# Attention plus MLP on one core: where a weight transfer is waited for, and which score product opens a filled half step

## The chip, the cores and the metric

The kernel runs on one core of a Trainium2 chip. The metric is the device time of one execution in microseconds (us), taken as the median of several runs; lower is better. The kernel before takes 1595.82 us (three runs, 1595.52 to 1599.61).

## The reference

One transformer block with a conditioning vector `c`, for 2048 rows of 512 numbers. Every head shares one key and one value of width 16 (multi-query attention, 32 heads).

```python
mod = (_silu(c) @ w_mod).reshape(c.shape[0], 6, 1, -1)
sa, ca, ga, sb, cb, gb = ...
h = _layernorm(x) * (1 + ca) + sa
q = (h @ wq) -> 32 heads of 16;  k = h @ wk;  v = h @ wv
scores = einsum("bhqd,bkd->bhqk", q, k) * (Dh ** -0.5)
x = x + ga * ((softmax(scores) @ v) @ wo)
h = _layernorm(x) * (1 + cb) + sb
x = x + gb * (gelu(h @ w1 + b1) @ w2 + b2)
```

## The kernel before

**Units and half steps.** The 2048 query rows are cut into 8 blocks of 256. A unit is one block and one group of four heads, so there are 64 units, worked through in order. For each unit every score is computed twice. A *max product* (`m`, line 490, in `Max.step`) is a score product whose 128x512 result VectorE reduces to a row maximum (line 495); a unit's maxima are found some units ahead and written into the unit's query tile as extra rows. An *exp product* (`e`, line 571, in `sexp`) is the same score with the maximum subtracted; ScalarE takes its exponential into `p` (line 572). Then `pv` (line 583) multiplies `p` by the values, for four heads side by side. One pass of the main loop does two key steps X and Y. It is cut in two halves, each a mix of score products closed by one `pv`; that stretch, from one `pv` to the next, is called a half step here. There are 512, and a counter `clock[0]` goes up by two in each (`due()` runs what was put off to a count by `later`).

**The two lanes.** A score product uses only 64 of TensorE's 128 rows: `s` = 0 or 1 names which. So each half step has two lanes, issued as two groups by `issue`: it always takes the next product of the group whose length so far is smaller, the first group on a tie. Each engine gets its instructions in exactly that written order (`manual_schedule`).

**Plain and filled half steps.** A plain half step (`plain`) has exp and max products in both lanes. A filled half step has four max and three exp products in one lane (call it A), and in the other (B) the halves of a batch of other work followed by the fourth exp product. That other work is the projections: `qps` for the queries, `wops` behind the attention, `tp` transposes, `w1ps` and `w2ps` of the MLP, all through `half` (line 183). A batch is split by rows, so the first half step of a pair runs the one 64-row half of it and the second the other. The second's group ends with `resume`, which lets the job that owns the batch go on: if an accumulation has ended, this writes the VectorE instruction that empties its PSUM bank. In the kernel before, where the batch ends an accumulation, the reduction of lane A's third max product is held back (`hold`) until `resume` has written that instruction.

**PSUM banks.** Max products rotate over three banks (tag `m`), so a max product must wait until the reduction of the one three before it is done. Exp products use three banks `e0`, `e1`, `e2`; lane A uses them in that order and lane B's exp product uses `e0` again, so it waits until the half step's first exponential is done.

**Weights of the MLP.** `fetch_w1` (line 732) moves one 512 KB piece of `w1` from DRAM into one of three buffers, by a DMA issued by SyncE. Three pieces are fetched ahead; piece f+3 is asked for one count after the last product of piece f. In the kernel before, the first product of a piece (in lane B) is what waits for it. One piece is used in each pair of half steps.

Of the kernel before, what the change touches and what calls it, by code (L numbers as in the profile page):

```python
# [11 lines left out]
ALU = mybir.AluOpType  # L12
AX = mybir.AxisListType

P = 128
# [27 lines left out]
def raw(ap):  # L43
    return ap.bitcast(F32)
# [3 lines left out]
def adaln_mqa_mlp(  # L48
# [15 lines left out]
    nc = tc.nc  # L64
# [41 lines left out]
    ks = const.tile([P, S], F32R, name="ks")  # L106
# [7 lines left out]
    dw1 = tc.dram_tile([NF, P, 2, KD, P], F32, name="dw1")  # L114
# [22 lines left out]
    clock = [0]  # L137
# [310 lines left out]
    NU = len(units)  # L448
    qsts = {}

    def load_q(u):

        b, Q = units[u]
        r0, w = blocks[b]
        qst = qsts[u] = qbufs[u % QBUFS]
        h, g, a0 = r0 // BQ, Q // 2, (Q % 2) * 2
        cols = slice(r0 % BQ, r0 % BQ + w)
        assert (h, g) in sent
        for s in range(2):
            for r, part in ((0, 0), (16, 1), (32, 0)):  # L460
                nc.sync.dma_start(out=raw(qst[64 * s + r:64 * s + r + 16]), in_=dq[h][g][part, a0 + s][:, :, cols])
            if u >= QBUFS:
                nc.sync.dma_start(out=raw(qst[64 * s + 48:64 * s + 50]), in_=dz)

    class Max:
# [14 lines left out]
        def has(self, s):  # L480
            return bool(self.todo[s])

        def step(self, s, hold=None, **place):
            u, j, t, kc = self.todo[s].pop(0)
            T = blocks[units[u][0]][1] // P
            if u not in self.mx:
                self.mx[u] = att.tile([P, 4 * T, NKC], F32, name=f"mx{u}", tag="mx", bufs=2)
            m = psum.tile([P, 512], F32, name=f"m{u}_{j}_{t}_{kc}_{s}", **(place or dict(tag="m", bufs=3)))
            rows = slice(64 * s, 64 * s + 64)
            nc.tensor.matmul(m, qsts[u][rows, j, t * P:(t + 1) * P], ks[rows, kc * 512:(kc + 1) * 512],  # L490
                             start=True, stop=True)
            i = (s * 2 + j) * T + t

            def reduce():
                nc.vector.tensor_reduce(out=self.mx[u][:, i, kc:kc + 1], in_=m, axis=AX.X, op=ALU.max)  # L495
                self.left[u] -= 1
                if self.left[u] == size[u] // 2 and u > 1 and u + 1 < NU:
                    load_q(u + 1)
                if self.left[u] == 0:
                    put_max(u, self.mx.pop(u))  # L500

            self.done += 1
            if hold is None:
                reduce()
            else:
                hold.append(reduce)

    placed = set()
    mms = []
# [44 lines left out]

    ptiles = {}
    accs = {}

    def sexp(u, K, j, s, bank):

        w = blocks[units[u][0]][1]  # L560
        qst = qsts[u]
        assert u in placed
        if (u, K) not in ptiles:
            ptiles[u, K] = att.tile([P, 2, 2, 512], F32, name=f"p{u}_{K}", tag="p", bufs=3)
        e = psum.tile([P, 512], F32, name=f"e{u}_{K}_{j}_{s}", tag="x" if bank == "x" else f"e{bank}", bufs=1)
        rows = slice(64 * s, 64 * s + 64)
        if w == 512:
            kt, rhs = K, qst[rows, j, :]
        else:
            kt, rhs = 2 * K + j, qst[rows].rearrange("p j n -> p (j n)")  # L570
        nc.tensor.matmul(e, ks[rows, kt * P:(kt + 1) * P], rhs, start=True, stop=True)  # L571
        nc.scalar.activation(ptiles[u, K][:, j, s, :], e, AF.Exp, scale=0.25)  # L572

    def pv(u, K):
# [154 lines left out]

    def fetch_w1(b, w1ts, f):  # L730
        w1ts[f] = wts_pool["rest"].tile([P, 2, KD, P], F32R, name=f"w1t{b}_{f}", tag="w1t", bufs=3)
        nc.sync.dma_start(out=raw(w1ts[f]), in_=dw1[f])

    def fetch_rest(b):

# [335 lines left out]
    held = []  # L1071

    def go_on(job):
        r = next(job[1], None)
        holder[:] = [job] if isinstance(r, list) or r is not None and r <= 0 else []
        if r is None:
            queue.remove(job)
        elif isinstance(r, list):
            held.append(r)
        else:  # L1080
            job[0] = clock[0] + max(abs(r), 1)
        return r is not None

    def resume():

        go_on(holder[0])
# [12 lines left out]
    def take():  # L1099
        advance()  # L1100
        return held.pop() if held else None

    size = [4 * (blocks[b][1] // P) * NKC for b, _ in units]
    first = [sum(size[:u]) for u in range(NU + 1)]
    mp = Max()
# [79 lines left out]
    rows = xhat1(1, act)  # L1185
# [49 lines left out]
    def products(batch):  # L1235

        return sum(b_.shape[-1] * (4 if b_.dtype == F32 else 1) for _, _, b_, _, _ in batch) / 512
# [7 lines left out]
    def issue(*groups):  # L1245

        at = [0.0] * len(groups)
        groups = [list(g) for g in groups]
        while any(groups):
            g = min((g for g in range(len(groups)) if groups[g]), key=lambda g: at[g])  # L1250
            length, fn = groups[g].pop(0)
            fn()
            at[g] += length

    def mixture(a, b):

        out = []
        while a or b:
            if a:
                out.append(a.pop(0))  # L1260
            if b:
                out.append(b.pop(0))
        return out
# [10 lines left out]
    for u in range(NU):  # L1274
        for K in range(0, steps[u], 2):
            goal = lead[u] + (lead[u + 1] - lead[u]) * (K + 2) / steps[u]
            goal = min(goal, first[u + QBUFS] if u + QBUFS < NU else first[NU])
            n = max(0, 2 * round((goal - mp.done) / 2))

            def maxes(s, n, first_=1.0, held=None):  # L1280
                return [(1.0 if i else first_, lambda i=i: mp.step(s, held if i == 2 else None)) if mp.has(s) else (0.0, lambda: None)
                        for i in range(n)]

            def exps(s, which):
                return [(1.0, lambda K=K, j=j, bank=bank: sexp(u, K, j, s, bank)) for K, j, bank in which]

            def halves(batch, s):

                total = products(batch)
                ahead = AHEAD if total > BATCH - 0.5 else (BATCH - (1.5 if batch[-1][4] else 0.5)) / total  # L1290
                return [(ahead * products([one]), lambda one=one: half(one, s)) for one in batch]

            def plain(s, K, t, n, banks):

                a, b_, c_, d = banks
                one = mixture(exps(s, [(K, 0, a), (K, 1, c_)]), maxes(s, n))
                other = maxes(t, n)
                if not holder and mp.has(t) and n > 1:
                    other[-1] = 1.0, lambda: mp.step(t, tag="x", bufs=1)
                issue(one, exps(t, [(K, 0, b_)]) + other + exps(t, [(K, 1, d)]))  # L1300

            X, Y = K, K + 1
            due()
            batch = take() if behind else None
            if batch:
                issue(mixture(maxes(1, n // 2, 0.0), exps(1, [(X, 0, 0), (X, 1, 1), (Y, 0, 2)])),
                      halves(batch, 0) + exps(0, [(X, 0, 0)]))
            else:  # L1310
                plain(1, X, 0, (n + 2) // 4, (1, 2, 0, 1))
            clock[0] += 1
            due()
            if behind:
                end_step(*behind)
            clock[0] += 1
            due()
            if batch:

                reduces = [] if batch[-1][4] else None  # L1320

                def go_on_():
                    resume()
                    for fn in reduces or ():
                        fn()

                issue(mixture(maxes(0, n // 2, 0.0, reduces), exps(0, [(X, 1, 0), (Y, 0, 1), (Y, 1, 2)])),
                      halves(batch, 1) + [(0.0, go_on_)] + exps(1, [(Y, 1, 0)]))
                advance()
            else:  # L1330
                plain(1, Y, 0, n // 4, (2, 0, 1, 2))
            clock[0] += 1
            due()
            end_step(u, X)
            behind = (u, Y)
            clock[0] += 1
            if state["mods"] and state["q"] == 0 and w2H is None:
                w2H = att.tile([P, NF, D], F32R, name="w2H", tag="bigH")
                w2L = att.tile([P, NF, D], F32R, name="w2L", tag="bigL")
                preps["w2"] = prep_w2()  # L1340
            if clock[0] >= prepared[0] + PREP and weights and weights[0] in preps:
                prepared[0] = clock[0]
                if next(preps[weights[0]], 0) == 0:
                    weights.pop(0)
# [51 lines left out]
```

## Time and profile before

| | us |
|---|---|
| median of the runs | 1595.82 |
| the profiled execution, whole | 1597.31 |
| its span on the core | 1595.0 |
| TensorE busy | 1569.6 |
| VectorE busy | 1410.1 |
| ScalarE busy | 1203.6 |
| GpSimd busy | 668.1 |

The span is the part between the first and the last instruction; 2.3 us of the profiled execution lie around it. In the profile PE is TensorE's matmuls, PEld its weight loads, PEq or PEldq its sequencer, DVE VectorE, ACT ScalarE, POOL GpSimd and SP SyncE. A row of the timeline gives start, duration, engine, line, operation, the output and inputs by the program's names, and shapes; "x2" means that two such instructions in a row are merged, and brackets give the idle time ahead of it with what ended it. Half steps run from about 79 us to 1540 us of the span.

### The profile page before, as it was taken

To read this page: it belongs to the slowest core of one execution; us is meant where nothing else is said; L and a number is where in the kernel's file an instruction comes from. 1 tells how busy PE (TensorE), PEld (TensorE's weight loads), DVE (VectorE), ACT (ScalarE), POOL (GpSimd) and SP (SyncE) were. 2 spreads that over 40 slices of the span, in tenths; PEclk is the share of its full clock that TensorE was granted. 3 is DMA by queue.
4 is the path that set the end of the run, shared out by engine and by line. 5 is a ranking of instruction groups with operands and counts; after the bars stand their busy time and mean duration, and the time that the engine had idled before them with its cause. 6 is when DMAs were issued, how large, how long until landed. Compare 5 with 4: busy or idle time off the path is not lost.

```text
span 1595.0 us, 41579 instructions
## 1 busy us (share of the span) xinstructions
PE 1569.6 (98%) x16369; PEld 1020.0 (64%) x16369; DVE 1410.1 (88%) x2473; ACT 1203.6 (75%) x2393; POOL 668.1 (42%) x1176
## 2 busy tenths in 40 slices
PE   6999999999999999999999999999999999999998
PEld 3466665557666676657666676656666676666667
DVE  6899999899989998999999999899999999999615
ACT  5577777778777887778877887778877887778853
POOL 4445443757412571246512562234602474225711
PEclk9999999999999999999999999999999999999999
DMA  7235312413021220303112120303112120211232
GB/s 242 88 109 198 121 65 70 133 32 108 14 78 51 60 78 26 102 19 106 32 48 80 54 85 22 105 15 98 43 36 91 43 97 18 95 40 61 83 132 74
DMA packets 83126, 121.62 MB, mean 76 GB/s; under 512 B 19614, under 2 KB 56222, under 8 KB 82676
## 3 DMA queue, kind: packets, MB, share of 16 engines
q1 hardware_dynamic: 82916, 118.97, 22.9%
q8 instruction: 129, 2.11, 0.6%
q14 instruction: 65, 0.53, 0.1%
q10 hardware_dynamic: 16, 0.00, 0.0%
HBM read 91.13 MB, written 27.27 MB: 74 GB/s over the span
## 4 chain that ended last, share of the span: by engine, by line
PE 92%; DVE 4%; ACT 2%; DMA 1%; POOL 0%; issue 0%; SPq 0%; ACTq 0%; DVEq 0%; POOLq 0%
PE acc L583 31%; PE m L490 25%; PE e L571 18%; PE w1ps L183 7%; PE w2ps L183 4%; DVE mx L495 3%; PE wops L183 1%; PE w2ps L177 1%; PE qps L183 1%; PE w1ps L177 1%; ACT p L572 1%; PE kps L159 1%; PE tp L183 1%; ACT h L838 0%; PE modr L279 0%; DMA wm<-in_w_mod_dram 0%
## 5 line engine op out<-in xcount | busy, mean ns | idle before, releaser
L495 DVE TENSOR_REDUCE mx<-m 128x1 f32<-128x512 f32 x2048 | 1269.0, 681 | 106.0 <-PE m L490 80.8
L572 ACT ACTIVATE p<-e 128x512 f32<-128x512 f32 x2048 | 1069.5, 599 | 307.5 <-PE e L571 237.1
L490 PE MATMUL m<-ks,qst 64*128 64x512 f32 x2048 | 820.4, 424 | 6.5 <-ACT ks L393 2.4
L571 PE MATMUL e<-qst,ks 64*128 64x512 f32 x2048 | 743.1, 407 | 2.9 <-ACT p L572 1.5
L583 PE MATMUL acc<-p,va 128*32 128x256 f32 x8192 | 548.0, 385 | 0.0
L490 PEld LDWEIGHTS m<-ks,qst 64*128 64x128 f32 x2048 | 362.7, 184 | 226.2 <-DVE mx L495 138.4
L571 PEld LDWEIGHTS e<-qst,ks 64*128 64x128 f32 x2048 | 365.9, 184 | 86.5 <-ACT p L572 59.0
L583 PEld LDWEIGHTS acc<-p,va 128*32 128x32 f32 x8192 | 213.8, 109 | 219.2 <-issue 115.8
L183 PE MATMUL w1ps<-h2H,w1t 64*128 64x256 f32 x1232 | 235.1, 287 | 0.0
L539 POOL TENSOR_SCALAR mt<-turned 8x32 f32<-8x32 f32 x256 | 53.5, 209 | 397.0 <-DVE turned L545 385.0
L183 PEld LDWEIGHTS w1ps<-h2H,w1t 64*128 64x128 f32 x1232 | 184.2, 185 | 0.0
L183 PE MATMUL w1ps<-h2L,w1t 64*128 64x256 f32 x616 | 169.7, 276 | 0.0
L183 PE MATMUL w2ps<-w2H,gH 64*128 64x512 f32 x286 | 117.8, 412 | 0.0
L183 PE MATMUL w2ps<-w2H,gL 64*128 64x512 f32 x286 | 117.3, 410 | 0.0
L183 PE MATMUL w2ps<-w2L,gH 64*128 64x512 f32 x286 | 117.3, 410 | 0.0
L183 PEld LDWEIGHTS w1ps<-h2L,w1t 64*128 64x128 f32 x616 | 113.5, 184 | 0.0
L891 POOL TENSOR_SCALAR tt<-tt 128x256 f32<-128x256 f32 x77 | 31.3, 406 | 163.0 <-ACT tt L890 159.5
L892 POOL TENSOR_TENSOR tt<-tt,z 128x256 f32<-128x256 f32 x77 | 57.0, 740 | 6.4
L134 POOL TENSOR_TENSOR gL<-z,gH 128x256 fp32r<-128x256 f32 x77 | 56.9, 739 | 6.4
L902 POOL TENSOR_TENSOR z<-tt,z 128x256 f32<-128x256 f32 x77 | 56.5, 734 | 6.0
L901 POOL TENSOR_TENSOR tt<-tt,z 128x256 f32<-128x256 f32 x77 | 56.7, 736 | 0.0
L183 PEld LDWEIGHTS w2ps<-w2H,gH 64*128 64x128 f32 x286 | 52.7, 184 | 0.6
(188 smaller groups left out, 1468.6 us busy)
## 6 DMA issues: line engine op xcount, KB each, us to landing
w1t<-dw SPq DMA_DIRECT2D x82, 512.0 KB
qst<-dq SPq DMA_DIRECT2D x384, 32.0 KB
do<-oc SPq DMA_DIRECT2D x64, 128.0 KB
dw<-w1s SPq DMA_DIRECT2D x11, 512.0 KB
xt<-in_A_x_dram SPq DMA_DIRECT2D x4, 1024.0 KB
dq<-qH SPq DMA_DIRECT2D x16, 256.0 KB
dq<-qL SPq DMA_DIRECT2D x16, 256.0 KB
x<-in_A_x_dram SPq DMA_DIRECT2D x8, 512.0 KB
```

The costliest lines, as they stand in the source:

```text
L134: eng_l.tensor_tensor(out=dst_l, in0=src, in1=raw(dst_h), op=ALU.subtract)
L177: nc.tensor.matmul(ps, a, b_, start=first_, stop=last_)
L183: nc.tensor.matmul(ps, a[rows], b_[rows], start=first_ and s == 0, stop=last_ and s == 1)
L490: nc.tensor.matmul(m, qsts[u][rows, j, t * P:(t + 1) * P], ks[rows, kc * 512:(kc + 1) * 512], start=True, stop=True)
L495: nc.vector.tensor_reduce(out=self.mx[u][:, i, kc:kc + 1], in_=m, axis=AX.X, op=ALU.max)
L539: nc.gpsimd.tensor_scalar(out=mt[:, g:g + 32], in0=turned[g:g + 4 * T, :], scalar1=1.0, scalar2=0.0, op0=ALU.mult, op1=ALU.add)
L571: nc.tensor.matmul(e, ks[rows, kt * P:(kt + 1) * P], rhs, start=True, stop=True)
L572: nc.scalar.activation(ptiles[u, K][:, j, s, :], e, AF.Exp, scale=0.25)
L583: nc.tensor.matmul(accs[u][32 * cidx:32 * cidx + 32, :], va[:, kt, :], rhs, start=kt == 0, stop=kt == NKT - 1)
L892: nc.gpsimd.tensor_tensor(out=tt, in0=tt, in1=z, op=ALU.mult)
L901: nc.gpsimd.tensor_tensor(out=tt, in0=tt, in1=z, op=ALU.mult)
L902: nc.gpsimd.tensor_tensor(out=z, in0=tt, in1=z, op=ALU.add)
```

## The change

Three things. First, lane A of a filled half step begins with an exp product and alternates exp, max, exp, max, exp, max, max; before, it was max, exp, max, exp, max, exp, max. Second, the holding back of a reduction is gone. Third, a transfer of a `w1` piece is noted with a count six higher than the present one (`heed`), and from that count on the next exp product with `s == 0` and an odd key step in the second half of a pair waits for it (`wait_early`), one transfer for each such product, in the order of the transfers.

```diff
-        def step(self, s, hold=None, **place):
+        def step(self, s, **place):
...
-            def reduce():
-                nc.vector.tensor_reduce(out=self.mx[u][:, i, kc:kc + 1], in_=m, axis=AX.X, op=ALU.max)
...
-            if hold is None:
-                reduce()
-            else:
-                hold.append(reduce)
+            nc.vector.tensor_reduce(out=self.mx[u][:, i, kc:kc + 1], in_=m, axis=AX.X, op=ALU.max)
...
+    def heed(dma, n):
+        heeded.append((clock[0] + n, dma.ins.name))
+
+    def wait_early(ins):
+        if heeded and heeded[0][0] <= clock[0]:
+            tc.add_manual_dep(ins.ins, heeded.pop(0)[1], ...)
...
-        nc.tensor.matmul(e, ks[rows, kt * P:(kt + 1) * P], rhs, start=True, stop=True)
+        ins = nc.tensor.matmul(e, ks[rows, kt * P:(kt + 1) * P], rhs, start=True, stop=True)
+        if clock[0] % 4 == 2 and s == 0 and K % 2:
+            wait_early(ins)
...
-        nc.sync.dma_start(out=raw(w1ts[f]), in_=dw1[f])
+        heed(nc.sync.dma_start(out=raw(w1ts[f]), in_=dw1[f]), 6)
...
-            def maxes(s, n, first_=1.0, held=None):
-                return [(1.0 if i else first_, lambda i=i: mp.step(s, held if i == 2 else None)) ...]
+            def maxes(s, n):
+                return [(1.0, lambda: mp.step(s)) if mp.has(s) else (0.0, lambda: None) for i in range(n)]
...
-                issue(mixture(maxes(1, n // 2, 0.0), exps(1, [(X, 0, 0), (X, 1, 1), (Y, 0, 2)])),
+                issue(mixture(exps(1, [(X, 0, 0), (X, 1, 1), (Y, 0, 2)]), maxes(1, n // 2)),
                       halves(batch, 0) + exps(0, [(X, 0, 0)]))
...
-                issue(mixture(maxes(0, n // 2, 0.0, reduces), exps(0, [(X, 1, 0), (Y, 0, 1), (Y, 1, 2)])),
-                      halves(batch, 1) + [(0.0, go_on_)] + exps(1, [(Y, 1, 0)]))
+                issue(mixture(exps(0, [(X, 1, 0), (Y, 0, 1), (Y, 1, 2)]), maxes(0, n // 2)),
+                      halves(batch, 1) + [(0.0, resume)] + exps(1, [(Y, 1, 0)]))
```

More of the change, by code (lines that the diff above doesn't have):

```diff
@@ L492, in step @@
             i = (s * 2 + j) * T + t
-            def reduce():
[L495 to L500, printed above, removed]
-            self.done += 1
-            if hold is None:
-                reduce()
-            else:
-                hold.append(reduce)
+            nc.vector.tensor_reduce(out=self.mx[u][:, i, kc:kc + 1], in_=m, axis=AX.X, op=ALU.max)
+            self.done += 1
+            self.left[u] -= 1
+            if self.left[u] == size[u] // 2 and u > 1 and u + 1 < NU:
+                load_q(u + 1)
+            if self.left[u] == 0:
+                put_max(u, self.mx.pop(u))
     placed = set()
@@ L556, in adaln_mqa_mlp @@
     accs = {}
+    heeded = []
+    def heed(dma, n):
+        heeded.append((clock[0] + n, dma.ins.name))
+    def wait_early(ins):
+        if heeded and heeded[0][0] <= clock[0]:
+            tc.add_manual_dep(ins.ins, heeded.pop(0)[1], mybir.DependencyInfo(mybir.DependencyClass.Sync, mybir.DependencyReason.DATA),
+                              reason="a weight piece")
     def sexp(u, K, j, s, bank):
@@ L1278, in adaln_mqa_mlp @@
             n = max(0, 2 * round((goal - mp.done) / 2))
-            def maxes(s, n, first_=1.0, held=None):
-                return [(1.0 if i else first_, lambda i=i: mp.step(s, held if i == 2 else None)) if mp.has(s) else (0.0, lambda: None)
-                        for i in range(n)]
+            def maxes(s, n):
+                return [(1.0, lambda: mp.step(s)) if mp.has(s) else (0.0, lambda: None) for i in range(n)]
             def exps(s, which):
@@ L1318, in adaln_mqa_mlp @@
             if batch:
[L1320 to L1325, printed above, removed]
-                issue(mixture(maxes(0, n // 2, 0.0, reduces), exps(0, [(X, 1, 0), (Y, 0, 1), (Y, 1, 2)])),
-                      halves(batch, 1) + [(0.0, go_on_)] + exps(1, [(Y, 1, 0)]))
+                issue(mixture(exps(0, [(X, 1, 0), (Y, 0, 1), (Y, 1, 2)]), maxes(0, n // 2)),
+                      halves(batch, 1) + [(0.0, resume)] + exps(1, [(Y, 1, 0)]))
                 advance()
```

## The prediction

> **What bounds the kernel now.** I read the page first: the engines' shares and the chain that ended last.
>
> ```profile
> PE 1569.6 (98%) x16369; PEld 1020.0 (64%) x16369; DVE 1410.1 (88%) x2473; ACT 1203.6 (75%) x2393; POOL 668.1 (42%) x1176
> ...
> PE 92%; DVE 4%; ACT 2%; DMA 1%; POOL 0%; issue 0%; SPq 0%; ACTq 0%; DVEq 0%; POOLq 0%
> ...
> L495 DVE TENSOR_REDUCE mx<-m 128x1 f32<-128x512 f32 x2048 | 1269.0, 681 | 106.0 <-PE m L490 80.8
> L572 ACT ACTIVATE p<-e 128x512 f32<-128x512 f32 x2048 | 1069.5, 599 | 307.5 <-PE e L571 237.1
> ```
>
> TensorE is the chain (92%), but VectorE is close behind it, nearly all of it reductions. A busy share can't say whether a half step is as short as TensorE can make it, so I went on to the windows of the `pv` line and then to the timeline of single half steps. First the rate, and a plain half step, which begins with exp products already:
>
> ```profile
> 600.00:800.00 200.00, 74.95 (x1120) 29.21 (x1120) 1.00 0.18 57
> ```
>
> ```profile
> 686.40 1.07 PE L583 MATMUL acc<-p,va 128*32 128x256 f32 x16
> 687.40 0.50 PE L571 MATMUL e<-qst,ks 64*128 64x512 f32 x2
> ...
> 689.01 0.42 PE L583 MATMUL acc<-p,va 128*32 128x256 f32 x4
> ```
>
> 1120 `pv` matmuls at 16 a half step are 70 half steps in 200 us, at a full granted clock (1.00). Six of them are plain; this one takes 689.01 - 686.40 = 2.61 us, and counting all six so the 64 filled ones take (200 - 15.7) / 64 = 2.88 us. Now a filled one, by engine:
>
> ```profile
> 802.90 1.07 PE L583 MATMUL acc<-p,va 128*32 128x256 f32 x16
> 803.90 0.50 PE L490 MATMUL m<-ks,qst 64*128 64x512 f32 x1
> 803.95 0.50 PE L183 MATMUL w2ps<-w2H,gL 64*128 64x512 f32 x1
> 804.24 0.39 PE L571 MATMUL e<-qst,ks 64*128 64x512 f32 x1
> ...
> 804.69 0.39 PE L571 MATMUL e<-qst,ks 64*128 64x512 f32 x1
> ...
> 805.15 0.66 PE L571 MATMUL e<-qst,ks 64*128 64x512 f32 x2
> 805.39 0.38 PE L490 MATMUL m<-ks,qst 64*128 64x512 f32 x1
> 805.74 0.84 PE L583 MATMUL acc<-p,va 128*32 128x256 f32 x10
> ```
>
> ```profile
> 804.43 0.69 DVE L495 TENSOR_REDUCE mx<-m 128x1 f32<-128x512 f32 x1 [0.35 <-PE w2ps L183]
> ```
>
> ```profile
> 804.66 0.60 ACT L572 ACTIVATE p<-e 128x512 f32<-128x512 f32 x1 [0.77 <-PE e L571]
> ```
>
> ```profile
> 805.18 0.18 PEld L490 LDWEIGHTS m<-ks,qst 64*128 64x128 f32 x1
> 805.31 0.18 PEld L571 LDWEIGHTS e<-qst,ks 64*128 64x128 f32 x1
> ```
>
> `pv` takes 1.00 us until the first score product; the second of lane A starts 0.34 later and the others every 0.23; 0.35 after the last start comes the next `pv`. That is 2.84 us, with little slack in two places. The fourth max product needs the bank of the first: product ends 804.40, reduction 804.43 to 805.12, weights loaded at 805.18, only 0.03 after the product ahead of it began, which is the earliest they can be. And lane B's exp product needs the first exponential: 804.66 to 805.26, weights at 805.31.
>
> **The change part by part.** In the written order VectorE, ScalarE and GpSimd keep every instruction in its place; only TensorE's order and its waits move. 436 of the 512 half steps are filled ones with max products, and all 436 change in the same way.
>
> *Exp first.* The entry costs the same with either product first: 1.00 us from `pv` in the plain half step and in the filled one. So nothing is won there. But the first max product moves to the second place, and the fourth stays last. The first then starts at 0.34 and ends 0.39 later (as the second product does now), at 0.73 from the first score product instead of 0.50; VectorE starts 0.04 behind it (804.40 to 804.43), at 0.77, and ends 0.69 later, at 1.46. The fourth's weights follow 0.06 behind (805.12 to 805.18): 1.51, where now they are loaded at 1.28. There are no more than three banks, so nothing hides this. A half step of before shows what it costs, one in which VectorE was late for another reason:
>
> ```profile
> 728.14 1.07 PE L583 MATMUL acc<-p,va 128*32 128x256 f32 x16
> 729.14 0.49 PE L490 MATMUL m<-ks,qst 64*128 64x512 f32 x1
> ...
> 731.07 0.42 PE L583 MATMUL acc<-p,va 128*32 128x256 f32 x4
> ```
>
> ```profile
> 729.91 0.69 DVE L495 TENSOR_REDUCE mx<-m 128x1 f32<-128x512 f32 x1 [0.17 <-PE e L571]
> ```
>
> ```profile
> 730.65 0.18 PEld L490 LDWEIGHTS m<-ks,qst 64*128 64x128 f32 x1
> ```
>
> Its reduction starts at 0.77, the weights are loaded at 1.51, and the next `pv` follows 0.42 later: 2.93 us. That is the new filled half step. The gain on the other side, exponentials 0.23 to 0.34 earlier and so lane B's exp product free at 1.18 instead of 1.41, lies beside the later end of lane A and is worth nothing. Against the mean of 2.88 the loss is 0.05 to 0.06 us x 436 = 24 us.
>
> *Knock-on.* Reductions that follow on one another take 1269.0 / 2048 = 0.62 us each. Four from 0.77 on (0.69 + 3 x 0.62) keep VectorE until 3.32, that is 0.39 into the next half step's products, and 0.38 more fits ahead of its first reduction without harm. Where a longer instruction comes in between, that reduction is late:
>
> ```profile
> L778 DVE BATCH_NORM_STATS2 st<-x 128x6 f32<-128x512 f32 x16 | 10.9, 682 | 0.1
> L938 DVE TENSOR_TENSOR ot<-w2ps,x 128x512 f32<-128x512 f32 x16 | 11.1, 691 | 23.6 <-PE w2ps L183 15.9 <-PE w2ps L177 7.8
> L771 DVE TENSOR_TENSOR x<-wops,x 128x512 f32<-128x512 f32 x16 | 11.0, 690 | 2.4 <-PE m L490 1.6 <-PE wops L177 0.8
> L441 DVE COPY q<-qps 128x512 f32<-128x512 f32 x14 | 9.7, 692 | 0.2
> ```
>
> ```profile
> 678.93 0.68 DVE L778 BATCH_NORM_STATS2 st<-x 128x6 f32<-128x512 f32 x1
> ```
>
> Before, four reductions from 0.53 on end at 3.08, 0.24 into the next products (half step 2.84); 0.68 for the instruction, 0.69 for the reduction and 0.06 give weights at 1.67. After it is 0.39 instead of 0.24: 0.15 later, where the main term has counted 0.055. So these 62 cases (one of them at 678.93) cost 0.095 more each: 6 us. It may be nothing, if VectorE catches up during work that it waits for, or 12, if each case delays a second half step.
>
> *The hold.* The reduction held back now stands behind what empties lane B's bank without it, since the third max product is itself written later; VectorE's order is unchanged: 0.
>
> *The early wait.* What it adds is a wait on an exp product; behind it stand the rest of the half step and `pv`, so a late piece would stop TensorE. When do pieces land?
>
> ```profile
> 553.53 0.28 PE L183 MATMUL w1ps<-h2L,w1t 64*128 64x256 f32 x1
> ```
>
> ```profile
> 556.82 3.20 SPq L732 DMA_DIRECT2D w1t<-dw  x2
> ...
> 1475.48 0.82 SPq L732 DMA_DIRECT2D w1t<-dw  x2
> ```
>
> ```profile
> 557.80:558.80 1.00, 1.00 (x16) 0.85 (x13) 0.54 (x2) 0.44 (x3) 0.83 (x3) 1.00 0.95 287
> 558.80:559.70 0.90, 0.90 (x14) 0.75 (x10) 0.90 (x2) 0.90 (x3) 0.62 (x1) 1.00 0.74 278
> ```
>
> Here the last product of a piece began at 553.53, and the next fetch into its buffer was issued at 556.82, since SyncE had other transfers to issue first. The two windows (DMA share 0.95 and 0.74, 287 GB/s for 1.0 us and 278 for 0.9) move 0.54 MB, a whole piece: it lands by about 559.8, 3.0 after its issue. The new wait stands seven counts after the asking, some 3.5 half steps or 10 us: 563.5. Slack 3.7 us even here. The worst is the pair at 1475.48 in the last block, which lands at 1478.5; its wait is the third score product of the half step at 1476.31 (below), so at 1476.31 + 1.00 + 0.57 = 1477.9: 0.6 us late, once. The rules of "DMA: Bandwidth & Descriptors" in the Trainium skill (section Rules for kernel authors) say to wait on a transfer's semaphore late; by that rule this part can only lose, and by the rows above it loses no more than that 0.6 us.
>
> What it takes away is a second wait at a piece's first product, handled by a sequencer instruction of its own:
>
> ```profile
> L183 PEldq EVENT_SEMAPHORE  x9: 51/51/51, 714.8 to 772.5; - x9
> ```
>
> ```profile
> 1476.31 1.07 PE L583 MATMUL acc<-p,va 128*32 128x256 f32 x16
> ...
> 1477.32 0.50 PE L183 MATMUL w1ps<-h2H,w1t 64*128 64x256 f32 x2
> ...
> 1479.16 1.07 PE L583 MATMUL acc<-p,va 128*32 128x256 f32 x16
> ...
> 1480.30 0.47 PE L183 MATMUL w1ps<-h2H,w1t 64*128 64x256 f32 x2
> ```
>
> A piece's first product starts 1.14 us after its `pv`, that of the other half 1.01 after: lane B loses 0.13. For about 59 pieces that is 0 to 8 us. I take 0, because lane A now ends later than lane B and covers it.
>
> Sum: 24 + 6 + 0 + 0 = +30 us. On the profiled execution 1597.31 becomes 1627.3; its own time is 1.5 above the median of the runs, so 1595.82 becomes 1626.
>
> **The rivals.**
>
> *Program order holds the max products (3%).* In 336 half steps lane B's exp product is now written ahead of the third and the fourth max product. If TensorE starts matmuls strictly as written, these two wait for it: it starts behind six halves, at 0.34 + 5 x 0.23 = 1.5, the third max product not before that, the last 0.23 later and `pv` another 0.35 later, at 2.08. That is 3.08 for the half step, 0.20 above today's: 67 us for these 336 and 6 for the other 100, so 1669. Against it: the first `w2ps` at 803.95 starts ahead of the exp product at 804.24, which is written before it. "TensorE: Matmul & The Clock Gate" in the Trainium skill (Part 3, What overlaps and what doesn't) has matmuls in strict order of start and end; this trace has them out of order between the two lanes.
>
> *VectorE's lateness adds up (12%).* If the 0.1 of the knock-on is the rule and not the exception, because the small reductions and copies push as well, the loss is 0.1 x 436 = 44 us: 1640. For it: VectorE's 88%. Against it: the longer half step leaves VectorE 0.38 us of air.
>
> *Exponentials decide, not banks: faster (7%).* The place is lane B's exp product, which waits for ScalarE at 1.41 today; in most half steps the fourth max product stands behind it in order. If that wait is what ends half steps, freeing it 0.23 earlier brings filled half steps from 2.88 towards 2.82 (1.00 + 0.34 + 5 x 0.23 + 0.33), and the early wait adds its 8 us on the w1 half steps: up to 26 + 8, and half of it gives 1579. This decides if the fourth max product's weights are loaded before 1.41; the bank's chain above gives 1.51.
>
> *Hidden (6%).* Lane B ends at 2.86 to 2.9 in w1 half steps anyway; if `pv` could start its own weights while the last max product streams, the delay would vanish: 1596. Against it stands the half step at 728.14.
>
> **How the numbers follow.** The forecast has 72%; the rivals have 12 (adding up), 7 (faster), 6 (hidden) and 3 (program order). The forecast's own range comes from the main term at 0.04 to 0.07 us (17 to 31), the knock-on's 0 to 12 and the early wait's -8 to +1: 1605 to 1640. To leave out no more than 2 in 10 I take 1607 to 1645, with the adding-up rival inside. A change of 0.3% (5 us) is about what can be told from none: faster 0.08, same 0.06, slower 0.86.
>
> **What would show it.** Right: rows of filled half steps with the first reduction 0.77 us after the first score product, the fourth max product's weights at 1.51, `pv` to `pv` at 2.93; 68 instead of 70 half steps in 200 us; VectorE's busy time unchanged and its idle time up by some 30 us; the first `w1ps` product of a piece 1.01 after `pv`; plain half steps at 2.61. Wrong: weights of the fourth max product at or below 1.41; an exp product idle for a DMA; `pv` above 3.0.

## The result, and the profile after

| | before | after |
|---|---|---|
| median of four runs each (us) | 1596.76 (1595.52 to 1599.61) | 1639.18 (1637.88 to 1640.67) |
| span of the profiled execution (us) | 1595.0 | 1635.6 |
| TensorE busy (us) | 1569.6 | 1607.8 |
| VectorE busy (us) | 1410.1 | 1412.1 |
| the 436 filled half steps, summed (us) | 1259.9 | 1303.8 |

The change makes the kernel slower: the ratio of the time after to the time before is 1.0263, with a 95% interval of 1.0245 to 1.0281. That is 42 us, where 30 were forecast. The last row is worked out from the `pv` rows of the two timelines. The filled half steps lose 43.9 us, so they hold all of the loss; the rest of the span is 3.3 us shorter. In the twelve traces of this document that rest lies between 331.1 and 336.7 us and goes with no part of the change; the time up to the first `pv` alone lies between 80.7 and 84.9 us.

The page of the changed kernel, its engines, the chain of waits and the group of reductions (in this kernel `pv` is line 588, the exp product 574, the reduction 493):

```profile
PE 1607.8 (98%) x16369; PEld 1025.2 (63%) x16369; DVE 1412.1 (86%) x2473; ACT 1224.4 (75%) x2393; POOL 665.1 (41%) x1176
...
PE 88%; DVE 7%; DMA 2%; POOL 1%; ACT 1%; issue 0%; SPq 0%; DVEq 0%; POOLq 0%; ACTq 0%
...
L493 DVE TENSOR_REDUCE mx<-m 128x1 f32<-128x512 f32 x2048 | 1277.9, 684 | 146.0 <-PE m L490 96.3
```

TensorE is still 98% busy, with 38 us more of it for the same 16369 matmuls. The busy share hides the loss: in the half step shown below no matmul has idle time ahead of it, but the fourth max product is busy for 0.47 us, where the one in the prediction's half step of before is for 0.38. What moved are the shares of the chain (VectorE 4% to 7%) and the idle time ahead of reductions (106.0 to 146.0 us). VectorE does the same work and waits 40 us longer for it.

The rate, from the windows of the `pv` line:

```profile
600.00:800.00 200.00, 72.90 (x1092) 28.38 (x1088) 1.00 0.17 56
```

1088 weight loads at 16 a half step are 68 half steps in 200 us, as forecast. One filled half step with `w1ps` work in lane B, on the timelines of TensorE, of its weight loads and of VectorE:

```profile
924.22 1.07 PE L588 MATMUL acc<-p,va 128*32 128x256 f32 x16
925.22 0.50 PE L574 MATMUL e<-qst,ks 64*128 64x512 f32 x1
...
925.56 0.39 PE L490 MATMUL m<-ks,qst 64*128 64x512 f32 x1
...
926.75 0.47 PE L490 MATMUL m<-ks,qst 64*128 64x512 f32 x1
927.15 1.07 PE L588 MATMUL acc<-p,va 128*32 128x256 f32 x16
```

```profile
926.73 0.18 PEld L490 LDWEIGHTS m<-ks,qst 64*128 64x128 f32 x1
```

```profile
925.99 1.29 DVE L493 TENSOR_REDUCE mx<-m 128x1 f32<-128x512 f32 x2 [0.34 <-PE m L490]
```

From the first score product at 925.22: the first max product starts at 0.34, its reduction at 0.77, and the weights of the fourth max product are loaded at 1.51. `pv` to `pv` takes 2.93 us. This is the chain of the prediction, number by number.

But 184 of the 436 have six 512-wide products in lane B (`qps`, `wops`, and half of `w2ps`), and these look different:

```profile
807.50 1.07 PE L588 MATMUL acc<-p,va 128*32 128x256 f32 x16
...
808.83 0.39 PE L490 MATMUL m<-ks,qst 64*128 64x512 f32 x1
808.84 0.39 PE L183 MATMUL w2ps<-w2H,gH 64*128 64x512 f32 x1
...
810.47 1.07 PE L588 MATMUL acc<-p,va 128*32 128x256 f32 x16
```

```profile
810.04 0.18 PEld L490 LDWEIGHTS m<-ks,qst 64*128 64x128 f32 x1
```

```profile
809.30 1.89 DVE L493 TENSOR_REDUCE mx<-m 128x1 f32<-128x512 f32 x3 [0.49 <-PE w2ps L183]
```

The max product ends at 809.22, at the same moment as a product of lane B that is written ahead of it, and the reduction starts 0.08 us later instead of 0.04. The weights follow at 1.54 and the half step takes 2.97 us.

One place was not in the sum at all. In the first block, an exp product stands idle for a weight piece (timeline of TensorE, then SyncE's queue, then windows with the busy time of PE, PEld, DVE, ACT and POOL, the granted clock, the DMA share and GB/s):

```profile
309.34 0.39 PE L183 MATMUL wops<-woL,onH 64*128 64x512 f32 x1
313.36 0.79 PE L574 MATMUL e<-qst,ks 64*128 64x512 f32 x1 [3.63 <-DMA w1t<-dw]
...
316.56 1.93 PE L588 MATMUL acc<-p,va 128*32 128x256 f32 x16
```

```profile
306.92 1.41 SPq L737 DMA_DIRECT2D w1t<-dw  x3
```

```profile
309.50:313.00 3.50, 0.23 (x1) 0.00 (x0) 0.69 (x1) 0.39 (x1) 3.33 (x4) 0.90 0.95 341
313.00:316.00 3.00, 2.64 (x8) 1.65 (x9) 1.29 (x2) 0.78 (x2) 2.83 (x4) 0.50 0.55 189
316.00:320.00 4.00, 4.00 (x28) 1.96 (x28) 1.76 (x3) 1.65 (x4) 0.41 (x1) 0.61 0.40 125
320.00:325.00 5.00, 5.00 (x54) 2.98 (x53) 4.99 (x9) 3.99 (x8) 0.00 (x0) 1.00 0.07 26
```

SyncE issues the first three pieces of the block together at 306.92, 1.5 MB. At 341 GB/s that is 4.6 us of transfer, with the DMA engines 95% busy. The exp product with the first wait would have started at about 309.57 (0.23 behind the product at 309.34), 2.7 us after the issue, and starts at 313.36. After that gap the granted clock is 0.50 and then 0.61, so the next products run slowly as well. The half step that ends at 316.56 lasts 8.80 us from its `pv` at 307.76, where 2.98 is typical of its kind, and the next one lasts 4.13.

### The profile page after: what moved, and what is told of

The parts are those of the page before. It is cut to its first block, busy times and chain, and to the rows that moved or that the text cites. A ratio compares the mean times of both kernels' runs of the same rounds, so it can differ in the third digit from the quotient of the medians.

```text
span 1635.6 us, 41520 instructions
## 1 busy us (share of the span) xinstructions
PE 1607.8 (98%) x16369; PEld 1025.2 (63%) x16369; DVE 1412.1 (86%) x2473; ACT 1224.4 (75%) x2393; POOL 665.1 (41%) x1176
## 4 chain that ended last, share of the span: by engine, by line
PE 88%; DVE 7%; DMA 2%; POOL 1%; ACT 1%; issue 0%; SPq 0%; DVEq 0%; POOLq 0%; ACTq 0%
PE acc L588 29%; PE e L574 24%; PE m L490 18%; PE w1ps L183 7%; DVE mx L493 5%; PE w2ps L183 3%; PE qps L183 2%; PE wops L183 1%; PE w2ps L177 1%; DMA xt<-in_A_x_dram 1%; PE w1ps L177 1%; PE kps L159 1%; PE tp L183 1%; DMA w1t<-dw 0%; DVE st L783 0%
## 5 line engine op out<-in xcount | busy, mean ns | idle before, releaser
L493 DVE TENSOR_REDUCE mx<-m 128x1 f32<-128x512 f32 x2048 | 1277.9, 684 | 146.0 <-PE m L490 96.3
L577 ACT ACTIVATE p<-e 128x512 f32<-128x512 f32 x2048 | 1091.1, 598 | 315.8 <-PE e L574 247.9
L574 PE MATMUL e<-qst,ks 64*128 64x512 f32 x2048 | 822.5, 427 | 4.3 <-DMA w1t<-dw 3.6
L490 PE MATMUL m<-ks,qst 64*128 64x512 f32 x2048 | 757.4, 423 | 7.5 <-DVE mx L493 2.4
L183 PEld LDWEIGHTS w2ps<-w2H,gL 64*128 64x128 f32 x286 | 52.8, 184 | 3.1
```

The source lines that it names most:

```text
L183: nc.tensor.matmul(ps, a[rows], b_[rows], start=first_ and s == 0, stop=last_ and s == 1)
L574: ins = nc.tensor.matmul(e, ks[rows, kt * P:(kt + 1) * P], rhs, start=True, stop=True)
```

## The experiments

Each time is a median; the kernel before was run beside each on the same chip (1597.31 for the first four, 1598.28 for the fifth to eighth, 1597.14 for the last two).

**Order alone.** The changed kernel without the early wait.

```diff
-        heed(nc.sync.dma_start(out=raw(w1ts[f]), in_=dw1[f]), 6)
+        nc.sync.dma_start(out=raw(w1ts[f]), in_=dw1[f])
```

> The changed kernel without the early wait: lane A begins with an exp product, nothing is held back, and a piece's first product waits for its transfer as before. Theory (the bank of the first max product sets the end of a filled half step): nearly all of the loss stays, since the reduction still starts 0.77 us after the first score product; the stall of some 5 us in the first block goes, and the second wait of a piece's first product comes back behind the longer lane A: 1632 to 1636. Rival (the early wait is the main cost): 1597 to 1605. Rival (it is half and half): about 1618.

Measured: 1633.64, ratio 1.0233 (1.0217 to 1.0248). The order costs 36 us of the 42, and the stall of the first block is gone.

**Wait alone.** The kernel before with `heed` and `wait_early`, in its old order.

```diff
+        ins = nc.tensor.matmul(e, ks[rows, kt * P:(kt + 1) * P], rhs, start=True, stop=True)
+        if clock[0] % 4 == 2 and s == 0 and K % 2:
+            wait_early(ins)
...
+        heed(nc.sync.dma_start(out=raw(w1ts[f]), in_=dw1[f]), 6)
```

> The kernel before with the early wait alone; order and hold as before. Theory: about 5 us lost where three pieces are asked for at once in the first block, and 59 half steps that get shorter by 0.065 us, 4 us: 1597 to 1600. Rival (the early wait is the main cost): 1630 or more. Rival (it is as good as free everywhere): 1592 to 1594.

Measured: 1598.88, ratio 1.0009 (0.9998 to 1.0021). This "nothing" is two effects of opposite sign. The 152 half steps with `w1ps` fall from a mean of 2.889 us to 2.861, 4.3 us in all; the 56 with `wops`, among them those of the first block, rise from 2.922 to 3.018, 5.4 us in all. The timeline of this kernel shows the same stall as the changed one (here the exp product is line 581):

```profile
309.34 0.79 PE L581 MATMUL e<-qst,ks 64*128 64x512 f32 x1 [4.19 <-DMA w1t<-dw]
```

**Half a reduction.** The changed kernel, with the first reduction of a filled half step made shorter.

```diff
-            nc.vector.tensor_reduce(..., in_=m, axis=AX.X, op=ALU.max)
+            nc.vector.tensor_reduce(..., in_=m[:, :cols], axis=AX.X, op=ALU.max)
...
-        nc.scalar.activation(ptiles[u, K][:, j, s, :], e, AF.Exp, scale=0.25)
+        nc.scalar.activation(ptiles[u, K][:, j, s, :], e, AF.Exp, scale=0.0005)
...
+            def maxes(s, n, cols=512):
+                return [(1.0, lambda i=i: mp.step(s, cols if i == 0 else 512)) ...]
```

The two filled calls pass `cols=256`.

> The changed kernel with one thing shorter: in filled half steps the reduction of the first max product reads 256 of its 512 columns. What it computes differs: that maximum covers half of its keys, and the exponential's factor is 0.0005 instead of 0.25, so that nothing overflows. Theory: the reduction takes about 0.42 instead of 0.69 us and frees the bank at 1.19 instead of 1.46; the fourth max product's weights are loaded by 1.3 and filled half steps fall to 2.83 to 2.88: 1580 to 1600. Rival (TensorE's written order or its queue sets the length, not VectorE): the time stays within 10 us of 1639.

Measured: 1595.32 (one run), where the changed kernel takes 1639.18. Its timelines of TensorE and of the weight loads:

```profile
918.74 1.07 PE L588 MATMUL acc<-p,va 128*32 128x256 f32 x16
919.74 0.50 PE L574 MATMUL e<-qst,ks 64*128 64x512 f32 x1
...
921.59 0.42 PE L588 MATMUL acc<-p,va 128*32 128x256 f32 x4
```

```profile
921.03 0.19 PEld L490 LDWEIGHTS m<-ks,qst 64*128 64x128 f32 x1
```

In the same written order the weights of the fourth max product are now loaded at 1.29 and the half step takes 2.85 us. TensorE's work was left as it was; the wait for the bank got shorter, and the loss went with it. VectorE also has some 0.26 us less to do in each of these half steps, so this run alone doesn't tell the bank from VectorE's load; the next one and the seventh move the bank's chain with VectorE's load unchanged.

**Max product third.** The order alone, with lane A written e e m m e m m, so that the first max product is one more place later.

```diff
-                issue(mixture(exps(...), maxes(1, n // 2)),
+                issue(pattern("eemmemm", e=exps(...), m=maxes(1, n // 2)),
```

> As the kernel with the order alone, but lane A runs exp, exp, max, max, exp, max, max: the first max product one place later still. Theory: its reduction starts at 1.00 instead of 0.77, so the fourth max product's weights are loaded at 1.74 and a filled half step takes 3.16: 0.23 x 436 = 100 us above the kernel with the order alone, 1720 to 1745. Rival (what costs is that an exp product opens the lane, or the two max products at its end): no more than 10 us above the kernel with the order alone.

Measured: 1729.99 (one run). TensorE, weight loads, VectorE:

```profile
977.53 1.07 PE L588 MATMUL acc<-p,va 128*32 128x256 f32 x16
...
979.11 0.39 PE L490 MATMUL m<-ks,qst 64*128 64x512 f32 x1
...
980.74 0.42 PE L588 MATMUL acc<-p,va 128*32 128x256 f32 x4
```

```profile
980.31 0.18 PEld L490 LDWEIGHTS m<-ks,qst 64*128 64x128 f32 x1 [0.22 <-DVE mx L493]
```

```profile
979.57 1.29 DVE L493 TENSOR_REDUCE mx<-m 128x1 f32<-128x512 f32 x2 [0.72 <-PE w1ps L183]
```

The first max product starts at 0.58 from the first score product at 978.53, its reduction at 1.04, the weights are loaded at 1.78, and `pv` follows at 3.21. This place costs another 96 us against the order alone, or 0.22 in each of the 436: nearly the whole 0.23 between two products of the lane.

**Lane B's second product behind the max product.** The changed kernel, with its stall, and one length changed in `halves`.

```diff
-                return [(ahead * products([one]), lambda one=one: half(one, s)) for one in batch]
+                lengths = [ahead * products([one]) for one in batch]
+                if products(batch[:1]) == 1:
+                    lengths[0] = 1.0
+                return [(length, lambda one=one: half(one, s)) for length, one in zip(lengths, batch)]
```

> The changed kernel, but where a lane B product is 512 wide the second one is written behind the first max product instead of ahead of it; each lane's own order stays. In the changed kernel the reduction starts 0.08 us after the first max product's end in those half steps, and 0.04 in the others. Theory (VectorE's wait counts what is written ahead on TensorE, and the lane B product that ends at the same instant holds it up): the reduction starts at 0.77 instead of 0.81 in the 184 half steps with six such products, 0.04 x 184 = 7 us less than the changed kernel: 1629 to 1635. Rival (the two lanes' simultaneous writes or the width itself make it late): 1637 to 1641.

Measured: 1633.26, ratio 1.0218 (1.0203 to 1.0232), where the changed kernel has 1.0263: 6 us less. TensorE and VectorE:

```profile
814.16 1.07 PE L588 MATMUL acc<-p,va 128*32 128x256 f32 x16
...
815.49 0.39 PE L490 MATMUL m<-ks,qst 64*128 64x512 f32 x1
...
817.09 0.42 PE L588 MATMUL acc<-p,va 128*32 128x256 f32 x4
```

```profile
815.92 0.69 DVE L493 TENSOR_REDUCE mx<-m 128x1 f32<-128x512 f32 x1 [0.46 <-PE m L490]
```

The two products still run side by side; only which of them is written first has changed. The reduction starts 0.04 us after the max product's end (815.88) and the half step takes 2.93 us. Over the whole trace the medians of the three kinds with six products fall from 2.98 to 2.94 us, and those of the others stay within 0.005.

**The wait, without the first block.** The kernel before with the early wait, except for the three pieces that are asked for together in the first block.

```diff
-        heed(nc.sync.dma_start(out=raw(w1ts[f]), in_=dw1[f]), 6)
+        dma = nc.sync.dma_start(out=raw(w1ts[f]), in_=dw1[f])
+        if b or f >= 3:
+            heed(dma, 6)
```

> The kernel before with the early wait, except for the three pieces that the first block asks for at once, which their first products wait for as before. Theory (those three alone make the early wait cost; all others shorten a half step, since a piece's first product has no second wait): 3 to 5 us below the kernel before, 1592 to 1594. Rival (the shorter half steps are taken back elsewhere): within 1 us of the kernel before. Rival (late pieces in other blocks): above it.

Measured: 1593.87 (9 runs), ratio 0.9972 (0.9960 to 0.9985). This version beats both kernels, by about as much as can be told from no change. The half steps with `w1ps` have a mean of 2.865 us instead of 2.889, and only 14 of the 152 are over 0.05 us above their median, where 59 were before.

**Max first, the rest as changed.** The order alone, with lane A written m e e m e m m: the old place for the first max product and a late place for the second and the third.

```diff
-                return [(1.0, lambda: mp.step(s)) if mp.has(s) else (0.0, lambda: None) for i in range(n)]
+                return [(1.0 if i or n < 3 else 0.0, lambda: mp.step(s)) if mp.has(s) else (0.0, lambda: None) for i in range(n)]
...
-                issue(mixture(exps(...), maxes(1, n // 2)),
+                issue(pattern("meememm", e=exps(...), m=maxes(1, n // 2)),
```

> As the kernel with the order alone, but lane A runs max, exp, exp, max, exp, max, max: the first max product is back in the first place, the end of the lane stays as in the changed kernel. Theory (only the place of the first max product counts): 1592 to 1602, as the kernel before. Rival (two max products at the end, or the exp product of lane B written ahead of them, cost as much as the opening): 1615 or more.

Measured: 1600.45 (10 runs), ratio 1.0016 (1.0006 to 1.0026). TensorE and VectorE:

```profile
992.82 1.07 PE L588 MATMUL acc<-p,va 128*32 128x256 f32 x16
993.83 0.50 PE L490 MATMUL m<-ks,qst 64*128 64x512 f32 x1
...
995.67 0.64 PE L588 MATMUL acc<-p,va 128*32 128x256 f32 x8
```

```profile
994.36 0.69 DVE L493 TENSOR_REDUCE mx<-m 128x1 f32<-128x512 f32 x1 [0.27 <-PE m L490]
```

The reduction starts at 0.53 and the half step takes 2.85 us. Moving one product back gives back 34 of the order's 36 us, so it is the first max product's place that counts and hardly that of the others.

**No hold.** The kernel before with `reduces = None`, so that no reduction is held back.

> The kernel before without the holding back: the third max product's reduction stands ahead of what empties lane B's bank. Theory: lane B's bank comes free up to 0.6 us later in the half steps that end an accumulation; the shorter of these instructions (0.48 us) are still done before the next half step needs the bank, the 46 long ones are not and delay it by up to 0.17: 0 to 8 us, 1597 to 1605. Rival (VectorE's order does not matter here): within 1 us of the kernel before.

Measured: 1597.94 (10 runs), ratio 0.9994 (0.9984 to 1.0003). The hold is worth nothing that can be measured, in either direction.

**The changed kernel, without the wait in the first block.** The same edit as in "The wait, without the first block", on the new order.

> The changed kernel with the early wait left out for the three pieces of the first block alone. Theory (those three make the early wait's cost, and elsewhere it is worth nothing here, since lane A ends later than lane B): 5 to 6 us less than the changed kernel, 1632 to 1635, as with the order alone. Rival (the other waits cost as well): 1636 to 1640. Rival (the other waits gain as they do in the order of before): 1629 to 1631.

Measured: 1633.16, ratio 1.0227 (1.0204 to 1.0250); the order alone took 1633.64. The interval is some 4 us wide to either side, so the times alone can't exclude the second rival. The traces can: the 152 `w1ps` half steps have a mean of 2.957 us here and 2.958 in the order alone. So outside the first block the early wait neither gains nor costs in this order. What it costs there is read from the `wops` half steps, whose mean is 2.995 us here and 3.109 in the changed kernel: 6.4 us over the 56.

**Lane B's exp product behind the third max product.** The order alone, with a length of 1.0 put behind the halves.

```diff
-                      halves(batch, 0) + exps(0, [(X, 0, 0)]))
+                      halves(batch, 0) + [(1.0, lambda: None)] + exps(0, [(X, 0, 0)]))
...
-                      halves(batch, 1) + [(0.0, resume)] + exps(1, [(Y, 1, 0)]))
+                      halves(batch, 1) + [(1.0, resume)] + exps(1, [(Y, 1, 0)]))
```

> The kernel with the order alone, but lane B's exp product is written behind lane A's third max product instead of ahead of it; each lane's own order stays. Theory: only the 28 w1 half steps whose third max product loads its weights at 1.30 or later gain by it, 0.08 each: 2 us less than with the order alone, 1630 to 1633, and in the profile those half steps take 2.94 instead of 3.02. Rival (the written order of the two lanes holds max products up in all half steps, as strictly ordered matmuls would): 10 us or more below the kernel with the order alone.

Measured: 1632.12, ratio 1.0218 (1.0195 to 1.0242). Against the order alone that is 1.5 us less, too little to tell from nothing. In the order alone, 28 of the `w1ps` half steps had the third max product's weights held to 1.30 or later, most of them to 1.37, behind lane B's exp product; in this one there are none, and the mean of the 152 falls from 2.958 to 2.945 us (2 us in all). Half of that is lost again in the 72 `w2ps` half steps with five products (2.950 to 2.966). The written order does move weight loads: in all kinds but that one the median of the third max product's is 1.18 to 1.19 in the order alone and 1.03 to 1.05 here. But the fourth waits for its bank until 1.51 or later either way, so the half steps get no shorter by it.

## Why the prediction was right, and where it was too small

**The mechanism was right.** The forecast was a loss through the bank of the first max product: reduction at 0.77, weights at 1.51, `pv` at 2.93. The rows of after show these numbers. Over the whole trace, the fourth max product's weights are loaded within 0.03 to 0.07 us of the end of the first reduction in 435 of the 436 half steps; before, in 117. Half a reduction takes the loss away, one place back takes away 34 of 36 us, and one place more adds 96. The other signs hold too: VectorE's busy time is unchanged (1410.1 to 1412.1) and its idle time up by 39 us, plain half steps stay at 2.61, and lane B begins 1.00 after `pv`.

**The main term was mis-sized: 24 us, where 42 were measured.** The step that failed reads "Against the mean of 2.88 the loss is 0.05 to 0.06 us x 436 = 24 us". It sets the new typical half step against the old mean, which has everything in it that makes half steps late. The prediction's own row had the old typical one, 2.84. Typical against typical, from all 436:

| lane B's work | half steps | median before | median after | difference x count |
|---|---|---|---|---|
| `w1ps` | 152 | 2.850 | 2.940 | 13.7 |
| `w2ps`, five products | 72 | 2.840 | 2.941 | 7.3 |
| `w2ps`, six products | 72 | 2.878 | 2.980 | 7.3 |
| `qps` | 56 | 2.882 | 2.983 | 5.7 |
| `wops` | 56 | 2.886 | 2.979 | 5.2 |
| `tp` | 28 | 2.844 | 2.947 | 2.9 |

That is 42.1 us, 0.09 to 0.10 in each kind. It is not 0.23, the distance between two places, because the weights had slack in the old order. The 1.28 of the prediction holds for the kind of half step that it showed. In all kinds but `w2ps` with five products, the fourth max product's weights were typically loaded at 1.41 already before, right behind those of lane B's exp product. A half step of this sort, on the timelines of TensorE and of the weight loads:

```profile
397.04 1.07 PE L583 MATMUL acc<-p,va 128*32 128x256 f32 x16
398.04 0.49 PE L490 MATMUL m<-ks,qst 64*128 64x512 f32 x1
...
399.89 0.42 PE L583 MATMUL acc<-p,va 128*32 128x256 f32 x4
```

```profile
399.45 0.18 PEld L571 LDWEIGHTS e<-qst,ks 64*128 64x128 f32 x1
399.46 0.18 PEld L490 LDWEIGHTS m<-ks,qst 64*128 64x128 f32 x1
```

The weights are loaded 1.42 after the first score product and the half step still takes 2.85 us. So a load at 1.41 costs next to nothing, and 1.51 costs the 0.10 beyond it.

The sums above these medians, the late half steps, are 12.4 us before and 14.2 after: they did not go away, as the use of the mean assumed. In the six-product kinds both medians have some 0.04 on top. After, it is the later reduction, which the prediction did not foresee and which the fifth experiment takes away. Before, lane B's first product started 0.05 to 0.07 us behind lane A's in these kinds (median) while the fourth max product started no later than in the others, so lane B seems to have ended the half step; why it starts late was not tried.

**The knock-on (6 us) is not there.** Without the first block's stall the late half steps sum to less than before, not more. First reductions more than some 0.15 behind the typical one are 14 after (later than 0.9) and were 32 before (later than 0.7). The prediction's lower end was right. Its reason, that VectorE catches up in the longer half step, fits these counts but was not tried by itself. So the 1640 of the rival "lateness adds up" is close to the measured time, but not by its mechanism. That the measured time lies within the forecast's range is luck in part as well: the main term (42) is above its bounds of 17 to 31 and the early wait (6) above its -8 to +1, and the late half steps, some 5 us less apart from the stall, took part of that back.

**The early wait (0) was wrong in one place.** The step reads "Slack 3.7 us even here", and then found one late pair, 0.6 us. It followed single pieces and pairs, each sent while one is used. The first three of the first block, asked for together, were left out, although the queue of before shows them:

```profile
303.19 1.41 SPq L732 DMA_DIRECT2D w1t<-dw  x3
```

After the change the first of the three is there 6.4 us after its issue (306.92 to 313.36), where the prediction's single piece took 3.0, and SyncE issues them about one half step ahead of the wait, not three and a half. The cost is about 6 us (1639.18 against 1633.16 without it). "Wrong: an exp product idle for a DMA" named this sign, and it came. The Trainium skill, "DMA: Bandwidth & Descriptors" (section Rules for kernel authors), would have a transfer waited for late; the first block agrees, while the sixth experiment shows a gain of 4 us from an earlier wait where the piece is there in time. What it gains is a piece's first product that has one wait instead of two, the relief of 0 to 8 us that the prediction named; taking it as 0 under the new order was right, since lane A covers it there.

**The hold (0)** was right: the traces have the same order of all 2473 VectorE instructions before and after. Strict program order of the products is not what TensorE does between the lanes: moving lane B's exp product in the written order changes the length of 28 `w1ps` half steps, not of 336. What it moves in the others are weight loads, which had time to spare.

Together: typical half steps 42.1, late ones 1.8 with the stall in them, and the rest of the span -3.3, is 40.6, the difference of the two spans.

## What to carry to other kernels

When buffers rotate, find the product whose buffer is wanted again last in a period, and count places from the first use to that return; moving the first use back costs a place in every period, less the slack that was left (here 0.10 us for the first place and 0.22 for the next), even on an engine that is 98% busy before and after. Set a typical period against a typical period, and count the late ones by themselves; a mean hides both. An earlier wait on a transfer is decided at the place where the most transfers are asked for together, and can be left out there alone.

## What was not expected of the hardware

**A short idle gap lowers the clock.** After 3.6 us without a matmul the granted clock was 0.50 for 3 us and 0.61 on average for the next 4, then 1.00. If it is 0.5 or 1, the full clock came back after some 3.1 of those 4 us, about 5.8 us after the first product. By the same reckoning the mean of 0.90 over 309.5 to 313.0 puts the fall to 0.50 at about 312.3, 2.6 us after the last matmul's end at 309.73. The Trainium skill, "TensorE: Matmul & The Clock Gate" (Part 1, What's actually happening), gives half the clock after at least one idle window of about 3.4 us and the full one after at least one busy window of that length; in this trace the fall came sooner after the last matmul than that, and the return took longer than one such window. The wait of 3.6 us made its half step 5.8 us longer than is typical (8.80 against 2.98), and the next 1.1 us.

**Two matmuls that end together delay what waits for the second.** A reduction starts 0.04 us after its product, and 0.08 when a product of the other lane that is written ahead of it ends at the same moment; turning the written order round gives the 0.04 back, some 6 us here. The Trainium skill, "TensorE: Matmul & The Clock Gate" (Part 3, The cost: per-tile semaphore tail), says that the semaphore increments of matmuls running together are written one after another, 26 ns each; the trace has 40 ns. Whether it is this that delays the reduction, or a wait that also counts the product written ahead, no run here separates.

**A second wait on one instruction is not free.** Giving one of a product's two waits to another instruction brought the `w1ps` half steps from a mean of 2.889 to 2.865 us, with the data there in time in both. Before, 57 of the 59 late ones among them hold a sequencer instruction for the second wait.
